# Block 0 of a pooled-attention and MLP kernel: v pooled on VectorE, u transposed by DMA, loads moved

## The chip, the cores and the metric

The kernel runs on one core of one Trainium2 chip. The time is that of the device for one execution in microseconds (us): the median of 3 runs before the change is 350.29 us (350.14 to 350.69). The profile is of one further execution; its span, from the first to the last instruction, is 347.7 us. Times with a position ("at 79.5") are us from the start of that span.

The core has five engines with a queue of instructions each, which wait for each other through semaphores: TensorE (PE: matmuls and transposes; the loading of its weights is listed apart as PEld), VectorE (DVE), ScalarE (ACT), GpSimd (POOL) and SyncE (SP, which here only issues DMAs). The DMA engines move data for all queues. SBUF is the on-chip memory; PSUM holds what TensorE writes.

## The reference, cut to what matters

Attention over keys and values that are means of 8 neighbours, followed by a residual MLP with token mixing:

```python
# q, k, v: (8 batches, 8 heads, 576, 64), f32
k_p = k.reshape(B, H, 72, 8, D).mean(axis=3)          # 576 keys become 72
v_p = v.reshape(B, H, 72, 8, D).mean(axis=3)
attn = softmax(q @ k_p^T / 8)                         # in the reference with max, exp, sum
x = (attn @ v_p), heads side by side                  # (8, 576, 512)

a1  = alpha1 * x + beta1
tok = einsum('ts,bsd->btd', w_tok, a1)                # w_tok 576 x 576 mixes the tokens
u   = x + lam * tok
a2  = alpha2 * u + beta2
ch  = relu(a2 @ w_ch1) @ w_ch2                        # 512 -> 2048 -> 512
out = u + lam * ch                                    # (8, 576, 512), f32
```

## The kernel before

The 8 x 576 rows of u are cut into 36 chunks of 128 rows, and the chunks into 9 blocks of 512 rows. Block n first runs 16 steps `mlp_A` (the first MLP matmul, one 128-column piece j of the 2048 at a time), then 16 quarter steps `mlp_B` (the second one, 4 chunks m of 4 parts). Meanwhile the attention of batch n+1 is woven in. Each piece of work of a block has a slot number; the pieces are issued in the order of these numbers. Slots 0 to 15 are mlp_A, 16 to 31 mlp_B. Batch 0's attention comes before block 0. Each engine runs its own instructions in this order.

```python
chunks: batch 0's four, batch 1's four, then the rest rows (512 to 575) of both as one; so for each pair
# block 0 = (0,0) (0,1) (0,2) (0,3); block 1 = (1,0) (1,1) (1,2) (1,3); block 2 = (0,4) (2,0) (2,1) (2,2); ...

for n in range(NBLK):
    todo  = [(j, mlp_A(n, j)) for j in range(0 if n else 4, 16)]
    todo += [(16 + 4 * m + part, mlp_B(n, m, part)) for m in range(4) for part in range(4)]
    # ... attention(n + 1), loads of batch n + 2 ...
    for _, do in sorted(todo, key=lambda x: x[0]): do()
```

The parts that matter here. Batch 1's v was loaded as f16 and pooled by TensorE; the later batches' v is loaded as f32, 72 partitions, and pooled by VectorE:

```python
def first_V(b, u, copy=nc.vector.tensor_copy):       # batches 0 and 1
    for c in range(4):
        nc.tensor.matmul(out=vp, lhsT=pool_v, rhs=main[:, heads, c], start=(c == 0), stop=False)     # L433
    for c in range(2):
        nc.tensor.matmul(out=vp, lhsT=pool_vr, rhs=rest[:, heads, c], start=False, stop=(c == 1))    # L435
    for r in range(2):
        copy(out=vp1_pool[2 * u + r][:, :, 0:64], in_=...)                                           # L438

def att_V(b, hp):                                     # batches 2 and on; two heads a call
    t = st1[b]["v"][hp // 2][:, 2 * (hp % 2):2 * (hp % 2) + 2]
    for n in (4, 2):
        nc.vector.tensor_tensor(out=t[:, :, 0:n], in0=t[:, :, 0:n], in1=t[:, :, n:2 * n], op=ALU.add)  # L445
    nc.vector.tensor_tensor(out=vp1_pool[hp][:, :, 0:64], in0=t[:, :, 0], in1=t[:, :, 1], op=ALU.add)  # L447
```

k of batches 1 and on is loaded as f32, summed by GpSimd (`sum_k`, L160 and L162, two of each per batch), pooled by TensorE (`att_K`) and cast to `kp` by VectorE (L419). The score matmuls (`att_S4`) need kp and q transposed, and give `ET`, the exponentials (ScalarE). `att_AV` multiplies ET with the pooled v, VectorE divides by the sum (L527, L529) into x, and `att_X` makes `xs`, x times lam and alpha1 in bf16.

Token mixing and the turn of u for the MLP:

```python
def mix_T(b, c, eng=nc.vector):
    # 5 (or 2 x 5) matmuls ps_tok <- wtT, xs                            L575
    # u = x + ps_tok (VectorE, L579); u_bf = u * alpha2 (eng, L582)

def mix_uT(key):
    if key[0] > 1 or key == (0, 4):
        nc.sync.dma_start_transpose(out=u_fm[blk][:, :, 128 * at:128 * at + 128], in_=s["u_bf"])     # L591
        return
    for cc in range(4):
        nc.tensor.transpose(out=ps_uT[...], in_=s["u_bf"][:, 128 * cc:128 * cc + 128], identity=...) # L596
    nc.scalar.copy(out=u_fm[blk][:, :, 128 * at:128 * at + 128], in_=ps_uT)                          # L598
```

`mlp_A(n, ·)` reads all four chunks of `u_fm[n]`. `setup_wtok_odd` makes the copy of the last rows of the mixing weights that odd batches use. q of batches 2 and on is transposed by DMA in `att_F` (two per batch); the last 64 rows of q and k ("rem") of each batch are loaded apart, cast by GpSimd (`cast_rem`) and q's are transposed in `att_Frem`. `keep_warm(n)` is n matmuls of 512 columns on zeros whose result nothing reads.

A DMA is issued with a destination buffer from a pool: k_raw and v_u have 2 buffers, q_bf 4. `behind` puts a small memset by an engine on the destination ahead of the load, so that the load starts no earlier than that engine gets there ("gated"). The order of the start-up part that the change touches:

```python
load_w1(0), load_w1(1), load_q_bf(1, 0), load_q_bf(1, 1), load_w1(2)          # GpSimd's queue
...
att_S(0, 5); first_V(0, 1); att_AV(0, 3); att_X(0, 2, 4, nc.gpsimd, False); load_al2(nc.vector)
att_S(0, 6); setup_vectors(); att_AV(0, 4); keep_warm(1); att_S(0, 7); att_AV(0, 5)
load_rem(1, behind=nc.vector)
... setup_wtok(0), setup_wtok(1), att_AV(0, 6), setup_rowsum(0), att_AV(0, 7)
load_k(1, 0), load_k(1, 1)                                                    # SyncE's queue, gated
...
load_w1(3); load_v16(1, (0, 1)); mix_T(0, 0); ...; load_v16(1, (2,)); load_w2(0); ...; load_w2(1), load_w2(2)
```

Of the kernel before, what the change touches and what calls it, by code (L numbers as in the profile page):

```python
# [23 lines left out]
def kernel(  # L24
# [27 lines left out]
    def gp(name):  # L52
        return psA.tile([P, 512], FP, tag="gp", name=name)
# [20 lines left out]
    def load_q_bf(b, u):  # L74

        bf = work.tile([P, 4, 4, D], BF, tag="q_bf", bufs=4, name="q_bf")
        nc.gpsimd.dma_start(out=bf.rearrange("p h c d -> p h (c d)"), in_=rows(q, b, u))
        st1[b]["q"][u] = bf

# [6 lines left out]
    def load_k(b, u, behind=None):  # L86
# [4 lines left out]
        nc.sync.dma_start(out=raw.rearrange("p h c d -> p h (c d)"), in_=rows(k, b, u))  # L91
        st1[b]["raw"][u] = raw

    def load_v16(b, parts=(0, 1, 2)):
# [32 lines left out]
    def load_v(b, u, parts=(0, 1), behind=None):  # L127

        if parts[0] == 0:
            st1[b]["v"][u] = work.tile([SPG, 4, 8, D], FP, tag="v_u", bufs=2, name="v_u")  # L130
        v_u = st1[b]["v"][u]
        if behind is not None:
            for rows_ in (slice(0, 64), slice(64, SPG)):
                behind.memset(v_u[rows_, 0, 0, 0:1], 0.0)
        for part in parts:
            g0, g1 = ((0, 64), (64, SPG))[part]
            nc.sync.dma_start(
                out=v_u[g0:g1].rearrange("g h p d -> g h (p d)"),
                in_=v[b, 4 * u:4 * u + 4, 8 * g0:8 * g1].rearrange("h (g p) d -> g h (p d)", p=8))

# [171 lines left out]
        nc.scalar.copy(out=wtT[64:65, 4, cols], in_=ps[64:65, 0:trc])  # L312

    def setup_wtok_odd():
        ps_w = gp("ps_wo").bitcast(BF)
        for tcx in range(5):
            trc = P if tcx < 4 else REM
            nc.tensor.transpose(out=ps_w[:, P * tcx:P * tcx + trc],
                                in_=wt_bf[0:trc, S * tcx + 448:S * tcx + 576],
                                identity=identity_bf[0:trc, 0:trc])  # L320
        nc.scalar.copy(out=wtT[:, 5, 0:S], in_=ps_w[:, 0:S])
        nc.scalar.copy(out=wtT[0:1, 5, 0:S], in_=wtT[64:65, 4, 0:S])


    w1 = [const.tile([P, 4, 512], BF, tag=f"w1_{g}", name=f"w1_{g}") for g in range(4)]
# [258 lines left out]
    def mix_uT(key):  # L584
        s = st2[key]
        i = where[key]
        blk, at = i // 4, i % 4
        if blk not in u_fm:
            u_fm[blk] = work.tile([P, 4, 512], BF, tag="u_fm", bufs=3, name="u_fm")
        if key[0] > 1 or key == (0, 4):  # L590
            nc.sync.dma_start_transpose(out=u_fm[blk][:, :, 128 * at:128 * at + 128],  # L591
                                        in_=s["u_bf"])
            return
        ps_uT = gp("ps_uT").bitcast(BF)
        for cc in range(4):
            nc.tensor.transpose(out=ps_uT[0:P, 128 * cc:128 * cc + 128],  # L596
                                in_=s["u_bf"][:, 128 * cc:128 * cc + 128], identity=identity_bf)
        nc.scalar.copy(out=u_fm[blk][:, :, 128 * at:128 * at + 128],  # L598
                       in_=ps_uT[:, 0:512].rearrange("p (c t) -> p c t", t=128))
# [109 lines left out]
    att_AV(0, 5)  # L709
    load_rem(1, behind=nc.vector)  # L710
    att_X(0, 4, 6, nc.gpsimd, False)
# [26 lines left out]
    mix_uT((0, 1))  # L738
# [12 lines left out]
    def attention(b):  # L751


        first = b == 1
        todo = []
        if first:
            for hp in range(4):
                todo.append((2.6 + 0.9 * hp, lambda hp=hp: att_F(b, hp)))
            todo.append((3.5, lambda: cast_rem(b, nc.gpsimd)))
            todo.append((3.65, lambda: load_w2(3)))  # L760
            todo.append((7.4, lambda: att_Frem(b, nc.scalar.copy)))
        if b < B - 1:
            at = 27.0 if first else 10.0
            todo.append((at, lambda: att_F(b + 1, 0)))
            todo.append((at + 0.1, lambda: att_F(b + 1, 2)))
            at = 28.0 if first else 25.5
            todo.append((at - 1.0, lambda: cast_rem(b + 1, nc.gpsimd)))
            todo.append((at, lambda: att_Frem(b + 1)))
        for u in range(2):
            todo.append((3.6 + 0.1 * u if first else -0.9 + 1.2 * u,  # L770
                         lambda u=u: sum_k(b, u, nc.gpsimd)))
            todo.append((6.4 + 1.8 * u if first else 4.1 + 2.0 * u,
                         lambda u=u: att_K(b, u, nc.vector.tensor_copy)))
            if first:
                todo.append((11.0 + 1.2 * u, lambda u=u: first_V(b, u)))
        for u in range(2):
            at = (9.0 if first else 6.3, 13.6)[u]
            todo.append((at, lambda u=u: att_S4(b, u)))
            for k, dt in enumerate((0.1, 0.1, 0.1, 0.7, 1.7, 1.75) if u else (0.1, 0.1, 0.1, 1.1, 2.1, 3.1)):
                todo.append((at + dt, lambda u=u, k=k: st1[b]["exp", u](k)))  # L780
            for i, dt in enumerate((2.9, 3.4, 4.6, 5.1) if u else (5.7, 6.2, 2.9, 3.4)):
                h = 4 * u + i
                todo.append((at + dt, lambda h=h: att_AV(b, h)))
                if i % 2:
                    eng = nc.gpsimd if h == 5 else nc.vector
                    todo.append((at + dt + 0.1, lambda h=h, eng=eng: att_X(b, h - 1, h + 1, eng)))
        if not first:
            for hp in range(4):
                todo.append((0.2 + 2.0 * hp, lambda hp=hp: att_V(b, hp)))
        for c in range(5):  # L790
            at = 21.0 + 1.3 * c
            if c < 4 or b % 2:
                todo.append((at, lambda c=c: mix_T(b, c)))
                key = (b, c) if c < 4 else (b - 1, 4)
                if first and c in (2, 3):
                    at += 1.3 * c - 2.0
                elif first and c < 2:
                    at += 1.0
                todo.append((at + 1.8, lambda key=key: mix_uT(key)))
        return todo  # L800

    for n in range(NBLK):
        todo = []
        for j in range(0 if n else 4, NJ):
            todo.append((j, lambda j=j: mlp_A(n, j)))
        for m in range(4):
            for part in range(4):
                at = 16 + 4 * m + part
                todo.append((at, lambda m=m, part=part: mlp_B(n, m, part)))
        if n == 0:  # L810
            todo.append((4.5, lambda: bias_row(1)))
            todo.append((6.2, lambda: setup_rowsum(4)))
            todo.append((8.3, setup_wtok_odd))
            for g in range(2, 4):
                todo.append((4 * g - 0.8, lambda g=g: setup_bias(g)))
        if n == NBLK - 1:
            for g in range(4):
                todo.append((2.0 + 3.0 * g, lambda g=g: scale_w2(g)))
        b = n + 1
        if b < B:  # L820
            todo += attention(b)
            if b + 1 < B:
                new_batch(b + 1)
                gate = nc.vector if b == 1 else None
                for u in range(2):
                    at = 21.0 + 0.2 * u
                    todo.append((at, lambda b=b, u=u: load_k(b + 1, u, gate)))
                    at = (21.0 if b == 1 else 0.4) + 0.1 * u
                    todo.append((at, lambda b=b, u=u: load_q_bf(b + 1, u)))
                    at = 19.0 + 0.2 * u if b == 1 else 3.5 + 4.0 * u  # L830
                    todo.append((at, lambda b=b, u=u: load_v(b + 1, u, behind=gate)))
                todo.append((20.9, lambda b=b: load_rem(b + 1, behind=gate)))
        for _, do in sorted(todo, key=lambda x: x[0]):
            do()

# [29 lines left out]
```

The softmax here doesn't subtract the row's maximum and nothing guards it: scores larger than these inputs give would overflow.

## Time and profile before

| what | value |
|---|---|
| time, median of 3 | 350.29 us (350.14 to 350.69) |
| span of the profiled execution | 347.7 us |
| granted TensorE clock | 1.000 |
| first half-width mlp_A matmul of block 0 | at 28.5 us |
| first mlp_A matmul of block 1 | at 71.8 us |
| ScalarE busy | 150.3 us |
| bytes read from HBM, written | 38.30 MB, 9.44 MB |

The profile names a group of instructions by engine, line of the kernel (L433), operation, tiles written and read, shapes and count. In a timeline the matmuls of a group are pipelined, so a group's length overlaps the next one's start: what it costs TensorE is the distance from its start to the next group's. In brackets stands how long the engine was idle before, and what it waited for. The slices of the whole page show DMA traffic by fortieths of the span: it is dense up to about 48 us, nearly absent to 58, and dense again to about 75.

### The profile page before, as it was taken

To read this page: it belongs to the slowest core of one execution; us is meant where nothing else is said; L and a number is where in the kernel's file an instruction comes from. 1 tells how busy PE (TensorE), PEld (TensorE's weight loads), DVE (VectorE), ACT (ScalarE), POOL (GpSimd) and SP (SyncE) were. 2 spreads that over 40 slices of the span, in tenths; PEclk is the share of its full clock that TensorE was granted. 3 is DMA by queue.
4 is the path that set the end of the run, shared out by engine and by line. 5 is a ranking of instruction groups with operands and counts; after the bars stand their busy time and mean duration, and the time that the engine had idled before them with its cause. 6 is when DMAs were issued, how large, how long until landed. Compare 5 with 4: busy or idle time off the path is not lost.

```text
span 347.7 us, 5897 instructions
## 1 busy us (share of the span) xinstructions
PE 336.4 (97%) x2208; PEld 178.9 (51%) x2249; DVE 219.8 (63%) x463; ACT 150.3 (43%) x283; POOL 89.7 (26%) x104
## 2 busy tenths in 40 slices
PE   8999999998999999999999999999999999999995
PEld 3667554454545554455445544554455445545544
DVE  6673159788686669775867597858685882037511
ACT  3656970257403850186018700790079005604700
POOL 8677404080117011800180027101600100000000
PEclk9999999999999999999999999999999999999999
DMA  8999953999558924895289628991820134011012
GB/s 123 184 219 243 214 115 44 239 240 196 93 178 152 222 48 112 216 201 86 77 235 175 113 72 208 197 139 53 221 69 1 37 85 77 0 60 62 0 58 63
DMA packets 66045, 44.57 MB, mean 128 GB/s; under 512 B 32409, under 2 KB 57309, under 8 KB 66018
## 3 DMA queue, kind: packets, MB, share of 16 engines
q1 hardware_dynamic: 50484, 33.18, 40.2%
q0 software_dynamic: 15072, 10.76, 21.1%
q8 instruction: 17, 0.28, 0.3%
q10 hardware_dynamic: 462, 0.27, 0.3%
q14 instruction: 10, 0.08, 0.1%
HBM read 38.30 MB, written 9.44 MB: 137 GB/s over the span
## 4 chain that ended last, share of the span: by engine, by line
PE 89%; DVE 4%; POOL 2%; DMA 2%; issue 2%; ACT 1%; POOLq 0%; DVEq 0%
PE ps_ch L646 34%; PE ps_h L612 33%; PE ps_tok L575 12%; PE ps_av L521 2%; PE ps_s L477 2%; DMA q_bf<-in_q_dram 2%; DVE v_u L445 1%; PE ps_ch L635 1%; DVE ps_ch L652 1%; PE ps_r L484 1%; PE ps_uT L596 1%; PE ps_av L525 1%; PE ps_kp L407 0%; PE ps_q L370 0%; DVE u_sb L653 0%
## 5 line engine op out<-in xcount | busy, mean ns | idle before, releaser
L617 ACT ACTIVATE Hj<-ps_h,bias_cols 128x512 bf16<-128x512 f32 x144 | 98.4, 689 | 149.1 <-PE ps_h L612 147.6
L612 PE MATMUL ps_h<-u_fm,w 128*128 128x512 bf16 (+1 forms) x571 | 132.2, 374 | 1.3 <-ACT u_fm L598 0.2
L646 PE MATMUL ps_ch<-w,Hj 128*128 128x512 bf16 x543 | 128.7, 379 | 1.1 <-issue 0.6
L612 PEld LDWEIGHTS <-w 128*128 128x128 bf16 x592 | 63.9, 114 | 51.8 <-issue 2.9
L646 PEld LDWEIGHTS <-Hj 128*128 128x128 bf16 x560 | 52.7, 98 | 61.0 <-issue 1.6
L575 PE MATMUL ps_tok<-xs,wtT 128*128 128x512 bf16 (+2 forms) x199 | 44.8, 380 | 0.5 <-DVE xs L543 0.2
L652 DVE TENSOR_TENSOR ps_ch<-lam_bc,ps_ch 128x512 f32<-128x512 f32 x32 | 22.2, 693 | 35.0 <-PE ps_ch L646 34.7
L543 POOL TENSOR_TENSOR xs<-x_tm,lamal_bc 128x512 bf16<-128x512 f32 x10 | 12.7, 1268 | 118.5 <-DVE x_tm L529 115.9
L579 DVE TENSOR_TENSOR u_sb<-x_tm,ps_tok 128x512 f32<-128x512 f32 (+1 forms) x40 | 27.4, 684 | 12.2 <-PE ps_tok L575 12.1
L529 DVE TENSOR_TENSOR x_tm<-ps_av,rec 128x320 f32<-128x320 f32 x64 | 31.4, 491 | 2.8
L653 DVE TENSOR_TENSOR u_sb<-u_sb,ps_ch 128x512 f32<-128x512 f32 x35 | 24.0, 687 | 13.7 <-PE ps_ch L646 12.5
L506 ACT ACTIVATE ET<-ps_s 72x512 f16<-72x512 f32 x56 | 32.3, 592 | 0.0
L527 DVE RECIPROCAL rec<-ps_av 128x5 f32<-128x5 f32 x64 | 12.2, 191 | 31.7 <-PE ps_av L525 31.6
L445 DVE TENSOR_TENSOR v_u<-v_u 72x512 f32<-72x512 f32 (+1 forms) x48 | 28.4, 591 | 0.8
L575 PEld LDWEIGHTS <-wtT 128*128 128x128 bf16 (+3 forms) x200 | 17.4, 100 | 20.9 <-issue 1.3
L582 DVE TENSOR_TENSOR u_bf<-u_sb,al_bc 128x512 bf16<-128x512 f32 x34 | 24.2, 711 | 1.3 <-DMA u_fm<-u_bf 0.2
L160 POOL TENSOR_TENSOR k_raw<-k_raw 128x512 f32<-128x512 f32 x14 | 19.3, 1376 | 11.9 <-DMA k_raw<-in_k_dram 9.4
L521 PEld LDWEIGHTS <-ET 72*128 72x128 f16 x256 | 13.9, 97 | 8.6 <-issue 0.4
L162 POOL TENSOR_TENSOR k_bf<-k_raw 128x512 bf16<-128x512 f32 x14 | 17.8, 1274 | 1.1
L543 DVE TENSOR_TENSOR xs<-x_tm,lamal_bc 128x512 bf16<-128x512 f32 x22 | 15.4, 701 | 0.7
L521 PE MATMUL ps_av<-vp,ET 72*128 72x66 f16 x256 | 15.8, 193 | 0.0
L145 POOL CAST rem_q<-rem_raw 128x256 bf16<-128x256 f32 x7 | 2.8, 399 | 42.0 <-DMA rem_raw<-in_q_dram 42.0
(121 smaller groups left out, 229.9 us busy)
## 6 DMA issues: line engine op xcount, KB each, us to landing
out_dram<-u_sb SPq DMA_DIRECT2D x32, 256.0 KB
k_raw<-in_k_dram SPq DMA_DIRECT2D x14, 512.0 KB
v_u<-in_v_dram SPq DMA_DIRECT2D x12, 512.0 KB
q_bf<-in_q_dram POOLq DMA_DIRECT2D x16, 256.0 KB, 6.5
w<-in_moe_w_ch_dram POOLq DMA_DIRECT2D x8, 512.0 KB, 16.3
v<-in_v_dram POOLq DMA_DIRECT2D x4, 256.0 KB, 11.2
rem_raw<-in_q_dram SPq DMA_DIRECT2D x15, 64.0 KB
rem_raw<-in_k_dram SPq DMA_DIRECT2D x15, 64.0 KB
```

The source lines that it names most:

```text
L445: nc.vector.tensor_tensor(out=t[:, :, 0:n], in0=t[:, :, 0:n], in1=t[:, :, n:2 * n], op=ALU.add)
L506: nc.scalar.activation(out=o, in_=i, func=AF.Exp, bias=0.0, scale=0.125)
L521: nc.tensor.matmul(out=av[:, odd + c, :], lhsT=ET[:, m0:m0 + 128], rhs=vp1[:, hh, :])
L529: nc.vector.tensor_tensor(out=x[:, 1 - odd:6 - odd, dd:dd + D], in0=av[:, :, 0:64], in1=rec.unsqueeze(2).to_broadcast((P, 5, D)), op=ALU.mult)
L543: eng.tensor_tensor(out=xs[:, 0:4, cols], in0=x[:, 1:5, cols], in1=lamal_bc[:, cols].unsqueeze(1).to_broadcast((P, 4, D * (h1 - h0))), op= ...
L575: nc.tensor.matmul(out=ps_tok[p0:p1], lhsT=wtT[0:kk, at, P * c:P * c + p1 - p0], rhs=xs_pool[i][0:kk, sc, :], start=(sc == 0), stop=(sc == 4))
L579: nc.vector.tensor_tensor(out=s["u"][p0:p1, :], in0=x[p0:p1, 1 + c if c < 4 else 5 - 5 * i, :], in1=ps_tok[p0:p1, 0:DM], op=ALU.add)
L582: eng.tensor_tensor(out=s["u_bf"], in0=s["u"], in1=al2_bc, op=ALU.mult)
L612: nc.tensor.matmul(out=ps_h[:, t0:t1], lhsT=w1_of(cc, j), rhs=u_fm[n][:, cc, t0:t1], start=(cc == 0), stop=(cc == 3))
L617: nc.scalar.activation(out=t, in_=ps_h, func=AF.Relu, bias=bias_cols[:, j:j + 1], scale=1.0)
L646: nc.tensor.matmul(out=ps, lhsT=Hj[n, j][:, 128 * m:128 * m + 128], rhs=w2[j // 4][:, j % 4, :], start=(j == 0), stop=(j == NJ - 1))
L652: nc.vector.tensor_tensor(out=ps, in0=lam_bc, in1=ps, op=ALU.mult)
```

## The change

All of it concerns what happens before and in blocks 0 and 1.

- Batch 1's v is loaded as f32 by GpSimd's queue, one DMA of 72 partitions for each half of the heads, and pooled by VectorE's att_V (slots 6.6, 8.7, 10.0, 12.6) instead of TensorE's first_V.
- Batch 1's u goes through the DMA transpose (the crossbar) instead of TensorE. So does the copy of the odd mixing rows: plain SBUF to SBUF copies by DMA.
- Batch 1's k is loaded earlier, by GpSimd's queue, in the place of the third part of w1, which moves back; the parts of w1, v and w2 are put in a new order.
- In block 0, the loads of batch 2 move from slots 19 to 21 to slots 14 to 14.6; its last rows are cast and transposed at 25.6 and 26.6 instead of 27 and 28, and its q at 28.5 instead of 27.
- In block 1, batch 3's q moves from slot 0.4 to 6.5 and its v from 3.5 to 6.7 (and 4 later), both behind a VectorE memset.
- Five keep_warm matmuls are added to the start.

```diff
-    load_w1(2)
+    for u in range(2):
+        load_k(1, u, queue=nc.gpsimd)
 ...
     att_S(0, 5)
+    keep_warm(1)
     first_V(0, 1)
+    keep_warm(1)
     att_AV(0, 3)
 ...
     att_S(0, 6)
+    keep_warm(1)
     setup_vectors()
     att_AV(0, 4)
+    keep_warm(2)
+    att_S(0, 7)
     keep_warm(1)
-    att_S(0, 7)
 ...
-    for u in range(2):
-        load_k(1, u, nc.vector)
 ...
-    load_w1(3)
-    load_v16(1, (0, 1))
+    load_w1(2)
+    for u in range(2):
+        load_v(1, u, (2,), queue=nc.gpsimd)          # part 2: all 72 partitions at once
     mix_T(0, 0, nc.gpsimd)
 ...
-    load_v16(1, (2,))
+    load_w1(3)
     load_w2(0)
     mix_T(0, 2, nc.gpsimd)
-    for g in range(1, 3):
-        load_w2(g)
+    load_w2(1)                                       # load_w2(2), (3) at slots 3.65, 3.75

 def setup_wtok_odd():
-    # 5 transposes by TensorE into ps_w
-    nc.scalar.copy(out=wtT[:, 5, 0:S], in_=ps_w[:, 0:S])
-    nc.scalar.copy(out=wtT[0:1, 5, 0:S], in_=wtT[64:65, 4, 0:S])
+    nc.vector.memset(wtT[0:64, 5, 0:S], 0.0)
+    nc.sync.dma_start(out=wtT[64:128, 5, 0:S], in_=wtT[0:64, 4, 0:S])
+    nc.sync.dma_start(out=wtT[0:1, 5, 0:S], in_=wtT[64:65, 4, 0:S])

 def mix_uT(key):
-        if key[0] > 1 or key == (0, 4):
+        if blk:

 # attention(b); first is b == 1
-            at = 27.0 if first else 10.0             # att_F(b + 1, 0), att_F(b + 1, 2)
+            at = 28.5 if first else 10.0
-            at = 28.0 if first else 25.5             # att_Frem; cast_rem one slot earlier
+            at = 26.6 if first else 25.5
-            todo.append((6.4 + 1.8 * u if first ...  # att_K(b, u)
+            todo.append((6.4 + 2.2 * u if first ...
-            if first:
-                todo.append((11.0 + 1.2 * u, lambda u=u: first_V(b, u)))
-        if not first:
-            for hp in range(4):
-                todo.append((0.2 + 2.0 * hp, lambda hp=hp: att_V(b, hp)))
+        for i, hp in enumerate((1, 0, 2, 3) if first else range(4)):
+            todo.append(((6.6, 8.7, 10.0, 12.6)[i] if first else 0.2 + 2.0 * hp, lambda hp=hp: att_V(b, hp)))
-                # batch 1's mix_uT up to 1.9 slots later than in other batches
+                # mix_uT at 1.8 after mix_T, as in other batches

 # loads of batch b + 1 in block b - 1
-                    at = 21.0 + 0.2 * u                                    # k
+                    at = (14.51 if b == 1 else 21.0) + 0.01 * u
-                    at = (21.0 if b == 1 else 0.4) + 0.1 * u               # q
+                    at = {1: 14.0, 2: 6.5}.get(b, 0.4) + 0.1 * u           # b == 2: behind a VectorE memset
-                    at = 19.0 + 0.2 * u if b == 1 else 3.5 + 4.0 * u       # v
+                    at = 14.55 + 0.01 * u if b == 1 else (6.7 if b == 2 else 3.5) + 4.0 * u   # b == 2 gated too
-                todo.append((20.9, ...load_rem(b + 1, behind=gate)))
+                todo.append((14.5 if b == 1 else 20.9, ...load_rem(b + 1, behind=gate)))
```

More of the change, by code (lines that the diff above doesn't have):

```diff
@@ L72, in rows, with load_q_bf @@
         return src[b, 4 * u:4 * u + 4, 0:512, :].rearrange("h (p c) d -> p h (c d)", c=4)
-    def load_q_bf(b, u):
+    def load_q_bf(b, u, behind=None):
         bf = work.tile([P, 4, 4, D], BF, tag="q_bf", bufs=4, name="q_bf")
+        if behind is not None:
+            behind.memset(bf[:, 0, 0, 0:1], 0.0)
         nc.gpsimd.dma_start(out=bf.rearrange("p h c d -> p h (c d)"), in_=rows(q, b, u))
@@ L84, in load_k16, with load_k @@
         st1[b]["k"][u] = t
-    def load_k(b, u, behind=None):
+    def load_k(b, u, behind=None, queue=nc.sync):
         raw = work.tile([P, 4, 4, D], FP, tag="k_raw", bufs=2, name="k_raw")
@@ L90, in load_k @@
             behind.memset(raw[:, 0, 0, 0:1], 0.0)
-        nc.sync.dma_start(out=raw.rearrange("p h c d -> p h (c d)"), in_=rows(k, b, u))
+        queue.dma_start(out=raw.rearrange("p h c d -> p h (c d)"), in_=rows(k, b, u))
         st1[b]["raw"][u] = raw
@@ L125, in load_rem, with load_v @@
         st1[b]["rem_raw"] = raw
-    def load_v(b, u, parts=(0, 1), behind=None):
-        if parts[0] == 0:
+    def load_v(b, u, parts=(0, 1), behind=None, queue=nc.sync):
+        if parts[0] != 1:
             st1[b]["v"][u] = work.tile([SPG, 4, 8, D], FP, tag="v_u", bufs=2, name="v_u")
@@ L135, in load_v @@
         for part in parts:
-            g0, g1 = ((0, 64), (64, SPG))[part]
-            nc.sync.dma_start(
+            g0, g1 = ((0, 64), (64, SPG), (0, SPG))[part]
+            queue.dma_start(
                 out=v_u[g0:g1].rearrange("g h p d -> g h (p d)"),
@@ L314, in setup_wtok_odd @@
     def setup_wtok_odd():
[L315 to L320, printed above, removed]
-        nc.scalar.copy(out=wtT[:, 5, 0:S], in_=ps_w[:, 0:S])
-        nc.scalar.copy(out=wtT[0:1, 5, 0:S], in_=wtT[64:65, 4, 0:S])
+        nc.vector.memset(wtT[0:64, 5, 0:S], 0.0)
+        nc.sync.dma_start(out=wtT[64:128, 5, 0:S], in_=wtT[0:64, 4, 0:S])
+        nc.sync.dma_start(out=wtT[0:1, 5, 0:S], in_=wtT[64:65, 4, 0:S])
     w1 = [const.tile([P, 4, 512], BF, tag=f"w1_{g}", name=f"w1_{g}") for g in range(4)]
@@ L759, in attention @@
             todo.append((3.5, lambda: cast_rem(b, nc.gpsimd)))
-            todo.append((3.65, lambda: load_w2(3)))
+            for u in range(2):
+                todo.append((3.65 + 0.1 * u, lambda u=u: load_w2(2 + u)))
             todo.append((7.4, lambda: att_Frem(b, nc.scalar.copy)))
         if b < B - 1:
-            at = 27.0 if first else 10.0
+            at = 28.5 if first else 10.0
             todo.append((at, lambda: att_F(b + 1, 0)))
             todo.append((at + 0.1, lambda: att_F(b + 1, 2)))
-            at = 28.0 if first else 25.5
+            at = 26.6 if first else 25.5
             todo.append((at - 1.0, lambda: cast_rem(b + 1, nc.gpsimd)))
@@ L771, in attention @@
                          lambda u=u: sum_k(b, u, nc.gpsimd)))
-            todo.append((6.4 + 1.8 * u if first else 4.1 + 2.0 * u,
+            todo.append((6.4 + 2.2 * u if first else 4.1 + 2.0 * u,
                          lambda u=u: att_K(b, u, nc.vector.tensor_copy)))
-            if first:
-                todo.append((11.0 + 1.2 * u, lambda u=u: first_V(b, u)))
         for u in range(2):
@@ L794, in attention @@
                 key = (b, c) if c < 4 else (b - 1, 4)
[L795 to L798, printed above, removed]
                 todo.append((at + 1.8, lambda key=key: mix_uT(key)))
@@ L825 @@
                 for u in range(2):
[L826 removed]
+                    at = (14.51 if b == 1 else 21.0) + 0.01 * u
                     todo.append((at, lambda b=b, u=u: load_k(b + 1, u, gate)))
[L828 to L832 removed]
+                    at = {1: 14.0, 2: 6.5}.get(b, 0.4) + 0.1 * u
+                    todo.append((at, lambda b=b, u=u: load_q_bf(
+                        b + 1, u, nc.vector if b == 2 else None)))
+                    at = 14.55 + 0.01 * u if b == 1 else (6.7 if b == 2 else 3.5) + 4.0 * u
+                    todo.append((at, lambda b=b, u=u: load_v(
+                        b + 1, u, behind=nc.vector if b < 3 else None)))
+                todo.append((14.5 if b == 1 else 20.9, lambda b=b: load_rem(b + 1, behind=gate)))
         for _, do in sorted(todo, key=lambda x: x[0]):
```

## The prediction

> **What bounds the kernel now.** I read the page's engine table and its chain of work first, then busy time by stage, then the timelines of single engines around each gap of TensorE.
>
> ```profile
> PE 336.4 (97%) x2208; PEld 178.9 (51%) x2249; DVE 219.8 (63%) x463; ACT 150.3 (43%) x283; POOL 89.7 (26%) x104
> PE 89%; DVE 4%; POOL 2%; DMA 2%; issue 2%; ACT 1%; POOLq 0%; DVEq 0%
> ```
>
> The first line is busy time by engine, the second the share of each engine in the chain that ended last. TensorE (PE) carries 97% and 89%. A part that is off TensorE counts only where TensorE waits for it; each matmul taken off its queue counts nearly in full.
>
> The next view is busy time by stage. A row has the stretch in us, its length, then each engine's busy us with instruction counts, the granted clock, the DMA share and GB/s. The cuts are the start of block 0's full-width MLP part, its second half, block 1, and block 2.
>
> ```profile
> 28.50:50.80 22.30, 21.62 (x217) 14.65 (x218) 5.91 (x16) 18.20 (x39) 7.57 (x9) 1.00 1.03 198
> 50.80:71.80 21.00, 20.74 (x133) 10.28 (x135) 16.86 (x38) 4.14 (x8) 4.77 (x6) 1.00 0.73 160
> 71.80:108.50 36.70, 35.29 (x222) 18.21 (x225) 27.47 (x52) 15.24 (x28) 14.29 (x14) 1.00 0.79 164
> 108.50:145.00 36.50, 36.13 (x231) 18.49 (x235) 27.55 (x55) 15.09 (x28) 9.67 (x11) 1.00 0.66 146
> ```
>
> Block 0 from 28.5 to 71.8 is 43.3 us; blocks 1 and 2 take 36.7 and 36.5. In block 0's first half VectorE (third figure) is busy 5.9 of 22.3 us, while ScalarE has 18.2 and the DMA engines are full (1.03). In its second half VectorE has 16.9 of 21.0. TensorE idles 1.4 us in block 1 and only 0.4 us in block 2.
>
> Where block 0's TensorE time goes, and its two gaps, in the TensorE timeline (start, length, line, operation, tiles, count, and in brackets the idle time before and its releaser):
>
> ```profile
> 39.48 0.29 PE L407 MATMUL ps_kp<-pool_main,k_bf 128*128 128x64 bf16 x4 [0.28 <-POOL k_bf L162]
> 39.66 0.52 PE L318 MATMUL ps_wo<-identity_bf,wt_bf 128*128 128x128 bf16 x5
> 40.11 1.05 PE L612 MATMUL ps_h<-u_fm,w 128*128 128x512 bf16 x4
> 43.56 0.60 PE L433 MATMUL ps_v<-v,pool_v 128*72 128x256 f16 x4
> 44.09 0.40 PE L435 MATMUL ps_v<-v,pool_vr 32*72 32x256 f16 x2
> 44.43 0.69 PE L351 MATMUL ps_bias<-b2c_bf,w 128*128 128x1 bf16 x16
> 64.65 0.39 PE L596 MATMUL ps_uT<-identity_bf,u_bf 128*128 128x128 bf16 x4
> 64.87 1.03 PE L646 MATMUL ps_ch<-w,Hj 128*128 128x512 bf16 x4
> 79.53 0.30 PE L477 MATMUL ps_s<-qT,kp 64*72 64x256 bf16 x2 [1.19 <-DVE kp L419]
> ```
>
> The cost of a group is read from start to start, as matmuls overlap: 39.66 to 40.11 is 0.45 us for the odd token-weight transposes, 43.56 to 44.43 is 0.87 us for one pooling of v, 64.65 to 64.87 is 0.22 us for one transpose of u.
>
> The 1.19 us gap waits for kp of batch 2, a VectorE cast at 79.03. VectorE's and GpSimd's timelines say why it is late:
>
> ```profile
> 73.34 3.12 DVE L445 TENSOR_TENSOR v_u<-v_u 72x512 f32<-72x512 f32 x2
> 76.49 1.25 DVE L447 TENSOR_TENSOR vp<-v_u 72x128 f16<-72x128 f32 x1
> 77.66 1.13 DVE L445 TENSOR_TENSOR v_u<-v_u 72x512 f32<-72x512 f32 x2
> 79.03 0.45 DVE L419 CAST kp<-ps_kp 128x288 bf16<-128x288 f32 x1
> 74.46 1.71 POOL L160 TENSOR_TENSOR k_raw<-k_raw 128x512 f32<-128x512 f32 x1
> ```
>
> The first pair of v sums took 3.12 us, the same pair later 1.13 us. In between GpSimd was still summing batch 2's k, since that k landed only at about 71.9.
>
> **What the skill says.** "SBUF — State Buffer", section "Who interferes with whom" (and the reading of the diagram before it): a VectorE operation with two SBUF inputs and a GpSimd operation that reads SBUF exclude each other for the whole instruction. The trace agrees: 3.12 against 1.13 us, and GpSimd's sum itself 1.71 instead of its usual 1.27. "DMA: Bandwidth & Descriptors", section "Issuing engines are not separate DMA queues": all queues share the same 16 engines, so moving k from SyncE's queue to GpSimd's adds no bandwidth; its section "DMA Transpose (X-bar)" lets only SyncE and ScalarE issue the plain transpose, for 2-byte data, which u_bf is. Here one such issue costs SyncE 1.2 us (for instance 1.22 us at 137.08), with the data down about 1 us later where the queues are empty. "TensorE: Matmul & The Clock Gate", section "Back-to-back issue gap": an isolated warm gap of N/2.4 ns plus 2.5, so 216 ns at 512 columns; twelve matmuls in 2.59 us at 54.23 agree, 0.216 us each.
>
> **The change part by part, on TensorE's clock.**
>
> 1. Batch 1's v is pooled on VectorE. Two groups leave TensorE: 0.87 + 0.86 (46.09 to 46.95) = 1.73 us saved. VectorE gets four att_V of 1.13 + 0.29, about 1.4 us each, 5.6 us in all, and loses four casts of 0.24. It has 16 idle us in that half, so this lies beside. The v loads are now f32 in 2 KB runs; GpSimd has already finished its k sums there, so they don't collide.
> 2. The odd token weights come by two SyncE copies and a VectorE memset: 0.45 us of TensorE saved, and 0.64 + 0.67 us of ScalarE copies.
> 3. Four u chunks of batch 1 go by DMA transpose: 4 x 0.22 = 0.88 us saved, and four ScalarE copies of 0.58 that lay beside.
> 4. Batch 1's k is issued at about 14 to 15.5 instead of 22.6, ahead of the third w1 part, so its sums end before 39.4: the 0.28 us gap goes. All weights move back by about one load. In the trace before, the last of w2 landed at 50.2 (15.0 after its issue at 35.2) against a need near 54; the total bytes are the same, so I take no new wait.
> 5. Batch 2's rem, k and v move from slots 19-21 to 14.5, some 9 us earlier. The DMA engines were idle there: 0.09 and 0.00 in the stretches 48-52 and 52-56. Then k of batch 2 is summed by GpSimd near 56 to 61, before att_V(2), so VectorE's first two att_V take 2.8 us instead of 5.7, kp comes 2.9 us earlier, and the whole 1.19 us gap goes.
> 6. Five more keep_warm matmuls at 16 to 19 us, four of them ahead of the last score matmul. ScalarE's last exp (18.75 to 19.46) waits for that matmul, the copies of wtT wait for the exp, the row sum and the last AV for those, and mix_T for the AV. So 4 x 0.216 = 0.86 us comes on top; the fifth lies in ScalarE's shadow.
> 7. Gating batch 3's loads to slot 6.5 keeps them behind the early transposes. It costs a few memsets of 0.06 us and removes no wait that I can see: 0.
>
> Sum: 1.73 + 0.45 + 0.88 + 0.28 + 1.19 = 4.53 saved, 0.86 added, net 3.67. From 350.29 that is 346.6. I add 0.2 for new collisions between the earlier k sums and VectorE's mixing phase, which is nearly full: **346.8**.
>
> **The rivals.**
>
> - *The crossbar becomes the wait.* Block 1 needs all four chunks of u at its first matmul. By TensorE's new clock it starts near 69.1. VectorE's last u_bf would be ready near 64, but SyncE issues in order: two transposes of u and the one of the rem rows stand ahead, 1.2 us each, so the last issue ends near 66.3 and lands near 67.5. The slack is under 2 us, and batch 2's loads, until about 62, share the DMA engines. If it is eaten, TensorE waits 1 to 2 us at block 1's start: 348 to 349. For it: the stretch 56-76 is full of DMA now; against it: those loads move away from it.
> - *VectorE becomes the bound in block 0's second half.* It is at 3.9 of 4 us from 60 to 64, and batch 2's k sums now fall on it; one such collision with a u_bf costs 0.43 us (1.12 instead of 0.69 at 142.28). Three or four would push xs and u_bf by 1.5 us: about 348.
> - *The keep_warms are free.* If TensorE's queue has hidden slack at 16 to 19 us, the 0.86 is not paid: 345.9. Against it: TensorE is busy 2.00 of 2.00 us from 16 to 18.
> - *A weight comes late.* w1's third part now stands behind k; if it lands past 37.5, block 0 waits: some 1 us worse.
>
> **Range and chances.** The savings that are whole instructions (3.06 us) are nearly sure; the two gaps (1.47) and the keep_warm cost are likely. All rivals against at once make about 349.5, all for it 345.3. Eight times in ten I expect 344.9 to 349.0. Over 2% faster would need 7 us, nearly twice what I can find: 0.04. Slower by 2% needs a stall of 10 us: 0.02. Within 2%: 0.94.
>
> **What would show it.** No ps_v of batch 1, ps_wo or late ps_uT on TensorE; its gap before batch 2's first score matmul gone, with the first v sums at 1.13 us; block 0 from its first full-width matmul to block 1's about 3.3 us shorter, with block 2 and on as long as before and only earlier. The first mix_T should start 0.8 us later than now (22.25). I'd be wrong if TensorE waits on u_fm at block 1's start, if VectorE waits for v in block 0, or if later blocks change in length.

## The result, and the profile after

The changed kernel takes 345.75 us (median of 4, 345.45 to 346.23); the kernel before beside it takes 350.25. The ratio is 0.987, with a 95% interval of 0.9853 to 0.9887. Run twice more beside the experiments, the changed kernel came out at 0.9913 (0.9899 to 0.9927) and 0.989 (0.9863 to 0.9918). So the gain is 3.3 to 4.5 us, some 1.1%.

The engine table and the chain that ended last, after the change:

```profile
PE 337.1 (98%) x2221; PEld 177.4 (52%) x2221; DVE 224.7 (65%) x476; ACT 146.9 (43%) x277; POOL 90.2 (26%) x105
PE 95%; DMA 2%; ACT 1%; DVE 1%; issue 0%; ACTq 0%; POOLq 0%
```

VectorE's share of the chain went from 4% to 1%, and TensorE's from 89% to 95%: most of what was left of waiting on VectorE is gone.

Busy time by stage, cut at the same events as before (first full part of block 0, its second half, block 1, block 2):

```profile
29.45:49.35 19.90, 19.59 (x203) 13.45 (x202) 10.57 (x31) 16.94 (x37) 9.12 (x11) 1.00 1.12 221
49.35:69.45 20.10, 20.10 (x121) 9.28 (x119) 18.36 (x33) 1.78 (x4) 8.62 (x8) 1.00 1.02 205
69.45:104.77 35.32, 35.32 (x226) 18.11 (x225) 25.26 (x58) 15.17 (x28) 8.31 (x10) 1.00 0.78 163
104.77:141.27 36.50, 36.50 (x236) 18.55 (x235) 27.30 (x55) 15.11 (x28) 9.76 (x10) 1.00 0.69 146
```

Block 0's halves are 19.9 and 20.1 us instead of 22.3 and 21.0, block 1 is 35.3 instead of 36.7, and block 2 is 36.50, as it was. VectorE (third figure) has taken on 4.7 us in the first half. The DMA engines are now full in the second half too (1.02, was 0.73).

By the positions of the first MLP matmul of each block, the account is as follows.

| stretch | before | after | difference | predicted |
|---|---|---|---|---|
| start to block 0's first mlp_A | 28.53 | 29.48 | +0.95 | +0.86 |
| block 0 | 43.27 | 39.96 | -3.31 | -3.34 |
| block 1 | 36.59 | 35.22 | -1.37 | -1.19 |
| blocks 2 to the end | 239.3 | 239.1 | -0.2 | 0 |

The TensorE lines that answer to those of before:

```profile
39.99 0.28 PE L404 MATMUL ps_kp<-pool_main,k_bf 128*128 128x64 bf16 x4
40.16 1.04 PE L609 MATMUL ps_h<-u_fm,w 128*128 128x512 bf16 x4
43.60 0.67 PE L348 MATMUL ps_bias<-b2c_bf,w 128*128 128x1 bf16 x16
75.66 0.28 PE L404 MATMUL ps_kp<-pool_main,k_bf 128*128 128x64 bf16 x4
75.91 0.30 PE L474 MATMUL ps_s<-qT,kp 64*72 64x256 bf16 x2
```

No idle time stands before ps_kp at 39.99; the MLP follows it directly, with no ps_wo between; no ps_v stands before ps_bias. Batch 2's first score matmul comes 0.25 us after ps_kp, where it had waited 1.19 us. VectorE and GpSimd around it and in block 0:

```profile
57.48 1.26 DVE L579 TENSOR_TENSOR u_bf<-u_sb,al_bc 128x512 bf16<-128x512 f32 x1
59.38 1.05 DVE L579 TENSOR_TENSOR u_bf<-u_sb,al_bc 128x512 bf16<-128x512 f32 x1
71.04 1.14 DVE L442 TENSOR_TENSOR v_u<-v_u 72x512 f32<-72x512 f32 x2
58.27 1.61 POOL L164 TENSOR_TENSOR k_bf<-k_raw 128x512 bf16<-128x512 f32 x1
```

The first pair of v sums is down from 3.12 to 1.14 us. The collision hasn't gone; it has moved to where it costs nothing: GpSimd now sums batch 2's k from 56.9 to 63, and three u_bf of VectorE took 1.26, 1.05 and 1.15 us instead of 0.69. No TensorE gap follows from it.

### The profile page after: what moved, and what is told of

It reads as the page before. It is cut to its first block, busy times and chain, and to the rows that moved or that the text cites. A ratio compares the mean times of both kernels' runs of the same rounds, so it can differ in the third digit from the quotient of the medians.

```text
span 343.8 us, 5902 instructions
## 1 busy us (share of the span) xinstructions
PE 337.1 (98%) x2221; PEld 177.4 (52%) x2221; DVE 224.7 (65%) x476; ACT 146.9 (43%) x277; POOL 90.2 (26%) x105
## 4 chain that ended last, share of the span: by engine, by line
PE 95%; DMA 2%; ACT 1%; DVE 1%; issue 0%; ACTq 0%; POOLq 0%
PE ps_h L609 36%; PE ps_ch L643 35%; PE ps_tok L572 11%; PE ps_s L474 2%; PE ps_av L518 2%; DMA q_bf<-in_q_dram 2%; PE ps_ch L632 1%; PE ps_kp L404 1%; PE ps_warm L563 1%; PE ps_q L367 1%; PE ps_sc L454 1%; PE ps_r L481 1%; PE ps_av L522 1%; PE ps_bias L348 0%; PE ps_bc L285 0%
## 5 line engine op out<-in xcount | busy, mean ns | idle before, releaser
L643 PE MATMUL ps_ch<-w,Hj 128*128 128x512 bf16 x560 | 130.9, 379 | 0.0
L609 PEld LDWEIGHTS <-w 128*128 128x128 bf16 x592 | 63.8, 114 | 51.7 <-issue 3.0
L572 PE MATMUL ps_tok<-xs,wtT 128*128 128x512 bf16 (+3 forms) x200 | 44.9, 380 | 0.3 <-DVE xs L540 0.3
L524 DVE RECIPROCAL rec<-ps_av 128x5 f32<-128x5 f32 x64 | 12.2, 191 | 32.5 <-PE ps_av L522 32.4
L442 DVE TENSOR_TENSOR v_u<-v_u 72x512 f32<-72x512 f32 (+1 forms) x56 | 30.8, 550 | 1.0
L579 DVE TENSOR_TENSOR u_bf<-u_sb,al_bc 128x512 bf16<-128x512 f32 x34 | 26.7, 785 | 1.7 <-DMA u_fm<-u_bf 0.6
L162 POOL TENSOR_TENSOR k_raw<-k_raw 128x512 f32<-128x512 f32 x14 | 18.3, 1310 | 9.1 <-DMA k_raw<-in_k_dram 6.5
L79 POOL DMA_DIRECT2D q_bf<-in_q_dram x16 | 12.6, 788 | 16.7 <-DVE v_u L136 15.2
## 6 DMA issues: line engine op xcount, KB each, us to landing
w<-in_moe_w_ch_dram POOLq DMA_DIRECT2D x8, 512.0 KB, 14.6
```

What stands on the lines that cost most here:

```text
L572: nc.tensor.matmul(out=ps_tok[p0:p1], lhsT=wtT[0:kk, at, P * c:P * c + p1 - p0], rhs=xs_pool[i][0:kk, sc, :], start=(sc == 0), stop=(sc == 4))
L579: eng.tensor_tensor(out=s["u_bf"], in0=s["u"], in1=al2_bc, op=ALU.mult)
L609: nc.tensor.matmul(out=ps_h[:, t0:t1], lhsT=w1_of(cc, j), rhs=u_fm[n][:, cc, t0:t1], start=(cc == 0), stop=(cc == 3))
L643: nc.tensor.matmul(out=ps, lhsT=Hj[n, j][:, 128 * m:128 * m + 128], rhs=w2[j // 4][:, j % 4, :], start=(j == 0), stop=(j == NJ - 1))
```

## The experiments

Each is compared with the kernel before, run beside it (349.97, 350.03 or 350.08 us). Since the executions start with a scatter (below), lengths of stretches in the trace are set against each other, not positions.

### The late loads, with u over the crossbar

```diff
 # the changed kernel, with:
-at = 28.5 if first ... ; at = 26.6 if first ...      # att_F, att_Frem of batch 2
+at = 27.0 if first ... ; at = 28.0 if first ...
-q, rem, k, v of batch 2 at 14.0, 14.5, 14.51, 14.55
+q, rem, k, v of batch 2 at 21.0, 20.9, 21.0, 19.0
```

> The changed kernel with batch 2's loads, casts and transposes back at their old slots (19 to 21, 27, 28). Theory (late k makes GpSimd's sums collide with VectorE's v sums, so kp is late): the first two v sums of batch 2 take about 3 us instead of 1.14 for the pair, a gap of 1.2 us before batch 2's first score matmul returns, block 0 itself keeps its length, time 346.9 to 347.1 us. VectorE's u_bf in block 0 fall from 1.05-1.26 back to 0.69 us without any gain in time. Rival (the gap in the kernel before came from VectorE's queue being late, not from the collision): the gap stays away, time within 0.3 us of 345.75. Rival 2 (late loads now delay the crossbar): block 1 starts later than 69.6.

Measured: 353.13 us, 0.9% slower than the kernel before (ratio 1.0089, 1.0064 to 1.0115), 6.4 to 7.4 us over the changed kernel. TensorE at block 1's start, and VectorE and SyncE (the lines whose engine is SPq are DMA issues):

```profile
75.13 6.37 PE L609 MATMUL ps_h<-u_fm,w 128*128 128x512 bf16 x20 [5.14 <-DMA u_fm<-u_bf]
63.58 0.69 DVE L579 TENSOR_TENSOR u_bf<-u_sb,al_bc 128x512 bf16<-128x512 f32 x1
65.14 0.99 SPq L93 DMA_DIRECT2D k_raw<-in_k_dram  x2
67.91 1.31 SPq L588 DMA_TRANSPOSE u_fm<-u_bf  x1
69.89 3.85 SPq L588 DMA_TRANSPOSE u_fm<-u_bf  x3
```

VectorE had u_bf of batch 1's last chunk ready at 64.3, but SyncE was still issuing batch 2's loads until 66.1, having waited 1.9 us ahead of the loads of k for a load of v to land, and it waited 1.8 us more for one ahead of the first transpose. The four transposes were issued from 67.9 to 73.7. TensorE idled 5.14 us, and then ran its first 20 matmuls in 6.21 us (75.13 to 81.34) instead of the 4.32 of the changed kernel (69.44 to 73.76), that is, at half clock at first (the granted clock was 0.50 from 73 to 79). Rival 2 of the expectation is right and its main theory wrong about block 0: **the early loads of batch 2 are what makes the crossbar affordable**, besides anything they do for k. The v sums took 1.13 us here too, since TensorE's and VectorE's standstill gave GpSimd time, so this run says nothing about the collision. VectorE's u_bf of batch 1 are back at 0.69 us, as the theory said.

### The early loads alone, in the kernel before

```diff
 # the kernel before, with batch 2's loads, cast_rem, att_Frem and att_F at the new slots;
 # u of batch 1 stays on TensorE, v and k of batch 1 as before
```

> The kernel before with one part of the change alone: batch 2's loads, casts and transposes at the new slots (14 to 14.6, 25.6, 26.6, 28.5); u of batch 1 still through TensorE. Theory (the gap of 1.19 us before batch 2's first score matmul comes from k sums that collide with v sums): gap gone, the first pair of v sums at 1.13 us instead of 3.12, block 0 as long as before (43.3 us within 0.2), block 1 at 35.2 instead of 36.6, time 348.7 to 349.1 against 350.25. Rival: the batch 2 loads fall on the time in which w2 still arrives and block 0 gets longer, gain under 0.5 us.

Measured: 349.36 us against 350.03 (0.9982, 0.9975 to 0.999). Three lines, TensorE at two gaps and VectorE:

```profile
39.92 0.29 PE L407 MATMUL ps_kp<-pool_main,k_bf 128*128 128x64 bf16 x4 [0.63 <-POOL k_bf L162]
78.72 0.30 PE L477 MATMUL ps_s<-qT,kp 64*72 64x256 bf16 x2
73.78 1.14 DVE L445 TENSOR_TENSOR v_u<-v_u 72x512 f32<-72x512 f32 x2
```

The first pair of v sums is at 1.14 us and the 1.19 us gap is closed, so its cause was the late k and the collision, as predicted. But the gain is only 0.67 us in time, short of the 1.15 or more that was expected. Block 1 is 35.85 us, 0.74 shorter instead of 1.4: a new 0.6 us stands at block 2's start, which the profile puts to "issue" (0.48), and its cause stays open. Block 0 is 43.62 us, 0.35 longer: the wait for k_bf of batch 1 is 0.63 instead of 0.28. That wait stands at 39.9, ahead of the moved loads (issued from 49.8), so it is not their work; it differs between executions (B below, with the same loads as the kernel before, has none). In the changed kernel batch 1's k comes earlier and neither wait is there.

### u of batch 1 on TensorE

```diff
 # the changed kernel, with:
-        if blk:
+        if key[0] > 1 or key == (0, 4):        # and the old slots of batch 1's mix_uT
```

> The changed kernel with batch 1's four u chunks transposed by TensorE again, at their old slots. Theory (TensorE pays whole instructions, the crossbar is in time): block 1 starts 0.88 us later, at 70.3 instead of 69.44, time 346.6 us. Rival (the crossbar's wait had eaten part of the gain): block 1 starts less than 0.4 us later. Rival 2 (the queue of SyncE is relieved too, so batch 2's q and rows come earlier and a later wait goes): blocks 1 and on get shorter by 0.2 or more.

Measured: 347.22 us (0.9917, 0.9894 to 0.9941). Block 0 is 40.85 us, 0.89 over the changed kernel's 39.96, and block 1 is 35.21. The four transposes cost what their starts say, and the crossbar takes nothing back. Rival 2 is wrong: the later blocks are not shorter.

### v of batch 1 on TensorE

```diff
 # the changed kernel, with batch 1's v as f16 and:
-            att_V(b, hp) at 6.6, 8.7, 10.0, 12.6
+            first_V(b, u) at 11.0, 12.2
```

> The changed kernel with batch 1's v loaded as f16 and pooled by TensorE again. Theory: block 0 longer by the two groups of 0.87 us, block 1 starts at 71.2 instead of 69.44, time 347.5 us. Rival (ScalarE or the DMAs set the pace of block 0's first half, so TensorE's saving was not all gain): block 1 starts less than 1.2 us later.

Measured: 347.81 us (0.9938, 0.9913 to 0.9962). Block 0 is 41.47 us, 1.51 over 39.96: most of the 1.73, between theory and rival. The changed kernel's second group of batch 1's score matmuls shows what was given back. In the changed kernel's TensorE timeline that group reads:

```profile
46.27 0.64 PE L474 MATMUL ps_s<-qT,kp 64*72 64x256 bf16 x2
46.64 0.26 PE L481 MATMUL ps_r<-rem_qT,kp 64*72 64x64 bf16 x1
...
47.33 1.05 PE L609 MATMUL ps_h<-u_fm,w 128*128 128x512 bf16 x4
```

In the kernel before it began and ended so:

```profile
48.08 0.30 PE L477 MATMUL ps_s<-qT,kp 64*72 64x256 bf16 x2
...
48.80 1.06 PE L612 MATMUL ps_h<-u_fm,w 128*128 128x512 bf16 x4
```

From its start to the MLP matmul behind it, it takes 1.06 us in the changed kernel, but 0.72 in the kernel before and 0.71 in this experiment. ScalarE's exponential of the first group runs from 46.01 to 46.59 in the changed kernel, and TensorE goes on at 46.64; before, that exponential had ended at 47.51, ahead of the group. So TensorE, with less to do, catches up with ScalarE and hands 0.35 us back. The coincidence of times speaks for this; no run changed that wait alone. Of the 0.35, 0.11 comes in again elsewhere: without the pooling ahead of it, the group ps_bias takes 0.53 us to the next start instead of 0.64.

### The odd mixing rows on TensorE

```diff
 # the changed kernel, with the old setup_wtok_odd (5 transposes, 2 ScalarE copies)
```

> The changed kernel with the odd mixing rows made by TensorE and ScalarE again (five transposes, two copies). Theory: block 0 longer by 0.45 us, 40.4 instead of 39.96, time 346.4 us against the changed kernel's about 346 on the same chip. Rival (ScalarE, which gets 1.3 us of copies back, sets the pace around 40 us): block 0 longer by 0.8 or more. Rival 2 (TensorE had slack there): under 0.2.

Measured: 346.52 us (0.9893, 0.9866 to 0.992), which the time alone can't tell from the changed kernel's 346.18 beside it. Block 0 is 40.61 us, 0.65 over 39.96: the 0.45 of the transposes, and 0.2 more, of which 0.17 lie at batch 1's first AV (0.30 us to its last matmul instead of 0.13). ScalarE's 1.3 us of copies just before are the likely reason; no run changed them alone.

### The gate of batch 3's loads

```diff
 # the changed kernel, with q of batch 3 at 0.4 and v at 3.5 (and 7.5), no memset ahead of them
```

> The changed kernel with batch 3's q and v loads at their old slots (0.4 and 3.5) and without the gate. Theory (the gate only keeps these loads behind the crossbar's transposes of batch 2, which have slack): GpSimd issues q of batch 3 at about 63 us, when its k sums are done, instead of 78, while u and q of batch 2 are on their way through the crossbar; the last u transpose lands up to 1 us later, block 1 starts within 0.3 us of the changed kernel's length of block 0 (39.96 us), time within 0.4 us of the changed kernel's. Rival (the crossbar is close to the path): block 1 waits for u_fm by 0.5 to 3 us, time 346.5 to 348.5. Rival 2: batch 2's q comes late through the crossbar and the gap stands in block 1, ahead of the first score matmul.

Measured: 347.00 us (346.21 to 347.69), the changed kernel beside it 346.76 (345.96 to 347.31): no difference that these runs resolve. Block 0 is 40.25 instead of 39.96, with the 0.29 at block 1's start, and block 1 is 35.20. That is at the edge of what the theory allowed; one profile gives the gate 0.29 us, and the times don't show it.

### The keep_warms, taken out and put in

```diff
 # A, the changed kernel without the five; C, with two of them (around first_V(0, 1))
-    keep_warm(1)                      # after att_S(0, 5)           A
-    keep_warm(1)                      # after first_V(0, 1)         A
-    keep_warm(1)                      # after att_S(0, 6)           A and C
-    keep_warm(2) ... keep_warm(1)     # around att_S(0, 7): one     A and C
+    keep_warm(1)                      # as in the kernel before
 # B, the kernel before with all five
```

A:

> The changed kernel without its five added keep_warm matmuls. Theory (they are pure cost, four of them on the chain through the last score matmul): block 0's first MLP matmul at 28.6 us instead of 29.48, everything after it earlier by 0.86, time 344.9 us. Rival A (they hold TensorE's clock up in the start): with them gone some stretch between 12 and 30 us runs at half clock, matmuls of 512 columns at about 0.43 us apart instead of 0.216, the first MLP matmul no earlier than 29.5, time 345.7 or more. Rival B (hidden slack in TensorE's queue): the first MLP matmul stays within 0.2 us of 29.48, time 345.6.

B:

> The kernel before with the five keep_warm matmuls alone. Where TensorE's clock stays full without them, they are pure cost: from the second q transposes to the first MLP matmul 15.9 us instead of 14.74, time 1.1 us longer. If, as in the run without them, a half-speed stretch of about 3 us comes in a good part of the executions of the kernel before, the median is less than 0.6 us above the kernel before, and its executions scatter less. The gap of 1.19 us in block 1 stays as it is in both cases.

C:

> The changed kernel with two of the five keep_warms (those around the second pooling of v) and without the other three. If two are enough to keep the clock up: no half-speed stretch, the ten transposes of the mixing weights take 0.57 us from start to next start, from the second q transposes to the first MLP matmul 15.2 us instead of 15.89, median 0.6 us below the changed kernel's on the same chip: the fastest of all. If not: the ten transposes at about 1.06 us and no gain.

The changed kernel beside C:

> The changed kernel again, beside the others on this chip. Expected 345.7 to 346.8 us, from the second q transposes to the first MLP matmul 15.9 us within 0.05.

| | time, us | ratio to the kernel before | second q transposes to first mlp_A | ten transposes of the weights | block 0 |
|---|---|---|---|---|---|
| kernel before | 350.08 | 1 | 14.74 | 0.56 | 43.27 |
| B, it with five keep_warms | 351.29 | 1.0037 (1.0021 to 1.0052) | 15.88 | 0.57 | 43.09 |
| changed, beside B and C | 346.18 | 0.989 (0.9863 to 0.9918) | 15.88 | 0.57 | 39.97 |
| A, changed without them | 346.25 | 0.9892 (0.9868 to 0.9916) | 15.81 | 1.06 | 39.97 |
| C, changed with two | 346.04 | 0.9872 (0.9847 to 0.9897) | 15.15 | 0.56 | 41.18 |

(A's ratio is to 349.97, the kernel before run beside it.) B settles the price: 1.14 us in the trace and 1.2 us in time. All five count, not four: in the changed kernel ScalarE waited from 20.11 to 20.25 for the weights' transposes, so the fifth didn't lie in its shadow. One expectation for B failed: the gap ahead of batch 2's first score matmul is 0.64 us, with 0.38 ahead of the pooling of k, instead of 1.19.

In the changed kernel, though, taking them out gained nothing that the times show. In A's profile the clock row and TensorE's timeline show a loss of the same size, with the ten transposes of the changed kernel below for comparison:

```profile
PEclk9989999999999999999999999999999999999999
20.44 1.26 PE L300 MATMUL ps_w<-identity_bf,wt_bf 128*128 128x128 bf16 x10
21.50 0.43 PE L518 MATMUL ps_av<-vp,ET 72*128 72x66 f16 x4
```

```profile
19.76 0.73 PE L300 MATMUL ps_w<-identity_bf,wt_bf 128*128 128x128 bf16 x10
20.33 0.28 PE L518 MATMUL ps_av<-vp,ET 72*128 72x66 f16 x4
```

The third slice (17 to 26 us) has a granted clock under 0.9, and the ten transposes take 1.06 us from start to start instead of 0.57. TensorE's clock had dropped to half from about 18.5 to 21.9 us, while the profile marks only 0.22 us of idle time between 13 and 20 us. That cost 1.07 us (15.81 against 14.74), about as much as the keep_warms.

It is tempting to conclude that the keep_warms hold the clock up, as rival A has it. **The other executions don't bear that out.** The profiled one has a mean granted clock of 0.995; A's five others have 1.000, so no such stretch, and still took 345.74 to 347.39 us instead of the expected 344.9. And the clock drops as well where the five are in: in B, 4 of 22 executions have 0.995 and are the longest four (352.92 to 353.37 us), as against 7 of 27 with 0.995 or less for the kernel before beside it; of the changed kernel's six there, one has 0.995 (348.38 us). Where in these executions it dropped is not on record. So what the five buy is not shown, and why A gained nothing in its other executions stays open: their start may have come later, or the weights may have held them up as in C below, and no trace is there to tell.

C's profile has no half-speed stretch (nor has that of the kernel before, with none of the five), and C got to block 0 earlier by 0.73 us. It lost that, and more, inside block 0:

```profile
53.06 2.75 PE L643 MATMUL ps_ch<-w,Hj 128*128 128x512 bf16 x12 [0.68 <-DMA w<-in_moe_w_ch_dram]
70.29 1.89 PE L609 MATMUL ps_h<-u_fm,w 128*128 128x512 bf16 x8 [0.22 <-DMA u_fm<-u_bf]
```

The issue of the last part of w2 and its time to landing, first in C and then in the changed kernel:

```profile
38.11 0.57 POOL L334 DMA_DIRECT2D w<-in_moe_w_ch_dram  x1
DMA to landing us min/median/max: 14.9/14.9/14.9
37.48 0.57 POOL L334 DMA_DIRECT2D w<-in_moe_w_ch_dram  x1
DMA to landing us min/median/max: 14.3/14.3/14.3
```

In C it landed at 53.0, when TensorE stood ready at 52.2; and the transposes of u, behind loads that came later too, cost another 0.4 at block 1. In the three profiles of the changed kernel it landed at 51.7 or 51.8 and was needed between 52.6 and 53.2. So **block 0 now runs only 0.8 to 1.5 us behind the weights**. But C would have been served in time by a landing at 51.8: its four parts of w2 all came 1.2 to 1.3 us later than in the changed kernel, and why is open. Whether a faster start is passed on when the weights come as usual, this profile can't say; the times of C and of the changed kernel beside it (346.04 and 346.18) don't differ clearly, where 0.6 us was expected.

### q of batch 1 over the crossbar too: an attempt to go on

```diff
 # the changed kernel, with:
-        if b > 1:                               # att_F: q by DMA transpose
+        if b:
-            todo.append((7.4, lambda: att_Frem(b, nc.scalar.copy)))
+            todo.append((4.0, lambda: att_Frem(b)))
```

> The changed kernel with batch 1's q (and its last rows) also transposed by DMA, as for later batches. Theory (whole TensorE instructions count, and SyncE's queue is empty from 30 to 48 us, so the crossbar is quick there although the DMA engines are busy): 16 transposes in four groups of 0.22 us and one of two at 0.10 leave, block 0 at 39.0 instead of 39.96, the wait in ScalarE's shadow at 46.3 shorter too, time 344.6 to 344.9 us. Rival (with the DMA engines full of weights, the transposes land late): TensorE waits for qT before batch 1's first score matmul at about 41 us, or the last part of w2 comes late at about 52, gain under 0.4 or a loss.

Measured: 358.66 to 366.93 us in six executions, median 364.32. The ratio of 1.0335 (1.0289 to 1.0382) is from the three shortest: a loss of about 12 us against the kernel before and of 15 against the changed one beside it. The rival is right, by far more than it said. The profiled execution is the shortest of the six; TensorE's gaps and SyncE's issues in it:

```profile
44.37 0.30 PE L474 MATMUL ps_s<-qT,kp 64*72 64x256 bf16 x2 [2.27 <-DMA qT<-q_bf]
49.46 0.29 PE L481 MATMUL ps_r<-rem_qT,kp 64*72 64x64 bf16 x2 [4.80 <-DMA rem_qT<-rem_q]
58.71 0.30 PE L474 MATMUL ps_s<-qT,kp 64*72 64x256 bf16 x2 [2.17 <-DMA qT<-q_bf]
32.17 1.18 SPq L380 DMA_TRANSPOSE rem_qT<-rem_q  x1
33.44 12.22 SPq L362 DMA_TRANSPOSE qT<-q_bf  x1
```

A transpose issued at 32.17 was down only at 49.4, 17 us later, and the issue of the next took SyncE 12.2 us, where the same instruction takes 1.2 to 1.6 in a quiet stretch. The DMA share was 0.96 to 1.43 throughout, from loads of GpSimd's queue, weights above all. SyncE's own loads had landed by then (the casts that wait for them start at 31.73 and 32.10), so what held the transposes up is likely the traffic of GpSimd's queue, perhaps with the first transpose of q, issued at 25.67, ahead of them; no run took either away.

### The changed kernel again

> The changed kernel itself, beside the others on this chip, for a median that can be compared. Expected 345.5 to 346.2 us; first MLP matmul of block 0 within 1 us of 29.5, block 0 39.96 and block 1 35.2 us long within 0.1.

Measured: 346.76 us (345.96 to 347.31), above the 346.2 expected at most, block 0 at 39.96 and block 1 at 35.20: the lengths repeat to 0.02 us. What scatters is the start. TensorE's pooling of batch 0's second half of k begins at 12.87, 13.36 and 13.46 us in the three profiles of the changed kernel, and between 12.55 and 14.78 over all runs here. The profile of the kernel before, at 12.55, is the earliest of all, which is why its span understates the gain (that execution took 349.43 us, where the median is 350.29).

No version tried is clearly faster than the changed kernel; C is level with it.

## Why the prediction was right, step by step

1. *v on VectorE*, 1.73: the work left TensorE as counted, and 1.51 of it arrived. The 0.35 handed back at the second score group wasn't foreseen.
2. *Odd mixing rows*, 0.45: 0.65; the extra 0.2 is likely ScalarE's relief.
3. *u over the crossbar*, 0.88: 0.89. The slack was there, but narrower than judged: the last issue ended at 67.5 instead of 66.3, and block 1 began at 69.44 instead of 69.1. Without the gate, or with the loads as late as in C, TensorE waited 0.3 to 0.4 us there. The rival was real, and the loads' new place kept it away.
4. *k early*, 0.28: gone, though no run moved k alone. "I take no new wait" for the weights held, with 0.8 us of slack in the profile compared: w2's last part landed at 51.8 against 52.6, since GpSimd issues it behind both k sums.
5. *Early loads*, 1.19: gone; block 1 is 1.37 shorter. The mechanism, k sums against v sums, is confirmed by the kernel before with the early loads alone, though there they gave only 0.67 us of time.
6. *keep_warm*, 0.86: the mis-sized term. It costs 1.14, since all five lie on the path. That the start came out at +0.95, near 0.86, is luck: the profile of the kernel before waits 0.36 us for q (at 13.79), and the changed kernel's doesn't. B confirms that they are a cost; why taking them out of the changed kernel (A) gained nothing, and what they do for the clock, stays open.
7. *The gate*, 0: 0.29 in one profile, nothing in the times.

Steps 1 to 4 give 3.34 against a measured 3.31 in block 0, partly since steps 1 and 2 are off in opposite ways. The 0.2 added for collisions wasn't needed: they came, three of about 0.45 us each, and VectorE absorbed them. The net of 3.67 lies within the 3.3 to 4.5 of three comparisons. One reading in the prediction is slightly off, without effect: the twelve matmuls given at 54.23 start at 54.06.

## What to carry to other kernels

A transpose by DMA takes work off TensorE, but it depends on what stands ahead of it in its queue and what else is on the way: the move saved 0.88 us of TensorE for u with the loads moved ahead, left TensorE idle for 5.14 us where they were not, and cost about 15 us for q while weights streamed in. So look at the queue first and then move the work. How busy the DMA engines are doesn't tell these apart by itself: their share was 0.75 to 1.70 from 58 to 68 us in the changed kernel, where the transposes came in time, and 0.96 to 1.43 from 32 to 50 with q's. When one engine is relieved, look for the wait just behind it (here 0.8 to 1.5 us to the weights, 0.35 us to ScalarE) before you relieve it further. And count filler matmuls as work, 1.14 us for five here; judge what they do for the clock over many executions, since one profile here showed a drop that five executions of the same kernel didn't have.

## What the runs showed of the hardware

- In one execution without the five keep_warms a half-speed stretch started amid short matmuls, with TensorE marked busy nearly throughout; "TensorE: Matmul & The Clock Gate", section "Why this matters for your kernels" of the Trainium skill, warns of idle gaps over about 3 us, and the 5.14 us gap with slow matmuls behind it (6.21 us for 20, not 4.32) agrees with it, but this stretch had no such gap.
- A DMA transpose of q took 12.2 us to issue and one of the last rows 17 us to land beside GpSimd's stream of weights.
- A 128x512 VectorE product with two SBUF inputs beside a GpSimd sum took 1.05 to 1.26 us instead of 0.69, in block 0 as the v sums did in block 1 before.
